# Two accumulator banks as two tiles instead of one in a fused recurrence and MLP kernel

## The chip, the cores and the metric

The kernel runs on one core of one Trainium2 chip. The metric is the device time of one execution in microseconds (us). The core has five engines that run side by side, each in its own order: TensorE (PE, matrix products), VectorE (DVE), ScalarE (ACT), GpSimd (POOL) and SyncE (SP, which issues most transfers). PE writes its products into an accumulator memory, PSUM, of eight banks; a bank holds 512 float32 numbers in each of 128 partitions. DVE and ACT read the products from there.

## The reference

Two blocks follow each other. The first is a gated linear recurrence over 768 tokens for 4 x 8 heads of width 48; the second is an MLP of 3072 tokens, 384 to 2048 to 384, with a quick GELU. All numbers are float32.

```
f = 1.0 / (1.0 + np.exp(-f_logit))
for t in range(S):
    state = f[:, :, t, :, None] * state + np.einsum('bhd,bhe->bhde', k[:, :, t], v[:, :, t])
    y[:, :, t] = np.einsum('bhd,bhde->bhe', q[:, :, t], state)
...
x = attn_out.transpose(0, 2, 1, 3).reshape(B * S, H * D)
h = x @ w_in
g = h * (1.0 / (1.0 + np.exp(-1.702 * h)))
return (g @ w_out).astype(np.float32)
```

## The kernel before

**Units.** The 3072 tokens are cut into twelve units (`NALL`) of 256 tokens (`U`), numbered 0 to 11. For each unit the kernel runs the recurrence ("attention") and then the MLP. The recurrence of a unit is done in chunks of 64 tokens: score products in six levels on PE (`score`, line 448), which DVE and ACT move under masks into a matrix A; then `add` (line 558) multiplies A with v into the accumulator y; the part "S" (line 669) makes the states at the chunk borders; the part "W" (line 716) adds what the states contribute to y. ACT then copies y to `yT` (line 731; line 768 in unit 11), transfers bring it into the layout `xT`, and POOL forms sums of it, called E (line 998).

**The MLP.** Units 0 to 2 run it with plain products. From unit 3 on its first layer (`mlp_h20`) is a scheme of twenty products for a 4 x 3 by 3 x 2 block product, with sums of blocks as operands. The table `PRODUCTS` names for each product its two operands, its parent (whose finished bank it adds onto) and the outputs it counts towards. `WHOLE` (units 3 to 10) and `HALVES` (unit 11, two groups) give the order on PE and put every product into a lane. `product` (line 1028) issues a product: PE at line 1036; a copy by ACT at line 1043 if a child goes on in another lane; then the reads: ACT at line 1055 for the first part of an output, DVE at line 1064 for the others, ACT at line 1051 where an output has a single part, and the GELU at line 1066. The second layer (`mlp_o7`, line 897, accumulators o_X, o_Y, o_Z, o_W) uses seven products in place of eight.

**PSUM.** All tiles come from one pool `ps`. Four tags, mm0 to mm3, hold one bank each; the function `bank` hands them out, and lanes 0 to 3 are these. The tag y is one tile of two banks, and so is sc. The tag y serves the scores of two levels in units 0 and 1, the accumulator of `add` in every unit (line 553, one bank for each group g of 128 tokens) and, in `mlp_h20`, lanes 4 and 5 (lines 1022 to 1025). The tag sc serves the scores, the state products, the last token's output (`y_last`, line 757), in unit 11 also lanes 6 and 7, and at the very end the product `o_last` (line 1161). A tile of a tag waits until the tile before it in the same tag has been read. In `mlp_h20` the lanes 4 and 5 of one unit are the two halves of one and the same tile:

```
tag = "y" if lane < 6 else "sc"
if tag not in shared:
    shared[tag] = ps.tile([P, 2, 512], F32, tag=tag, name=f"h_{n}_{tag}")
banks[lane] = shared[tag][:, lane % 2, :wide * w].rearrange("p (t x) -> p t x", x=w)
```

**What sets the order.** The orders of PE and POOL are written out by hand for the whole kernel (line 91): from unit 3 on, the parts of the next unit's attention are merged into the MLP's list of products by their widths. For units 0 to 2 the orders of all engines are written out (`fill_order`, closed at line 1386). After that the framework sets the order of DVE, ACT and SP at build time, by its own estimate of when each instruction can start, and it derives all semaphore waits from the tiles that instructions read and write. `half` copies y to `yT`: half(0) reads the bank of group 0 and a part of the other, half(1) the rest, later. In unit 11 fifteen operations on DVE (line 1103) and one at line 1101 build `sum_last`, the output of the last token, which PE turns over in `o_last` (line 1162). In attention, z (line 629) is the transpose of k that goes out to memory and comes back as `kt`, and ACT turns it into `kn` (line 644) for the products at line 669. The DVE transposes at line 367 bring in the next unit's inputs, and the products on X at line 546 scale them for each level.

Of the kernel before, what the change touches and what calls it, by code (L numbers as in the profile page):

```python
# [9 lines left out]
F32 = mybir.dt.float32  # L10
# [13 lines left out]
def kernel(  # L24
# [33 lines left out]
    nc = tc.nc  # L58
# [29 lines left out]
    wp = ctx.enter_context(tc.tile_pool(name="wp", bufs=2))  # L88
    mlp = ctx.enter_context(tc.tile_pool(name="mlp", bufs=2))
    ps = ctx.enter_context(tc.tile_pool(name="ps", bufs=1, space=bass.MemoryType.PSUM))  # L90
    ctx.enter_context(tc.manual_schedule(engines={mybir.EngineType.PE, mybir.EngineType.Pool}))
    fill_order = ExitStack()
    fill_order.enter_context(tc.manual_schedule())
# [244 lines left out]
    def attention(n):  # L338
# [124 lines left out]
        def columns(h, g):  # L463

            return rows(h ^ g)

        def scores(tag="sc"):
            new = ps.tile([P, 2, NP, 2, HS], F32, tag=tag, name=f"sc_{n}_{next(serial)}")
            t["sc"], t["both"] = (new[:, 0], new[:, 1]), [(0, new.rearrange("p h a s t -> p (h a) s t"))]
            return new  # L470

# [78 lines left out]
        def add():  # L550


            t["py"] = ps.tile([P, NG, NP, 2, HS], F32, tag="y", name=f"y_{n}")
            for a in range(NP):
                for f in (1, 0):
                    for h, g in TILES:
                        to, w = (slice(0, HS), HS) if h == g == 0 else (columns(h, g), D)
                        nc.tensor.matmul(
                            t["py"][to, g, a, f, :],
                            lhsT=vts[n][g * HS:(g + 1) * HS, f, (2 * a + h) * D:(2 * a + h) * D + w],  # L560
                            rhs=A[g * HS:(g + 1) * HS, h * NP + a, f, :],
                            start=(f == 1 and a == 0), stop=False, skip_group_check=True,
                        )
# [47 lines left out]
        def turn_k(a0):  # L611
            if a0 == 0:
                new_kn()
            if n < N_FILL + 1:
                pt = bank([P, 2, 2, P], f"tkn_{n}_{a0}")
            else:
                pt = ps.tile([P, 2, 2, P], F32, tag="sc", name=f"tkn_{n}_{a0}")
            for a in range(2):
                for f in range(2):
                    x = (a0 + a) * HALF  # L620
                    nc.tensor.transpose(pt[:, a, f, :], slot((KR, KF)[f])[:, x:x + HALF], ident)
            nc.scalar.copy(t["kn"][:, a0:a0 + 2], pt)
# [33 lines left out]
        @part("S")  # L656
        def _():
            if n:
                add()
                pd = scores().rearrange("p h a s t -> p h (a s t)")  # L660
                pd = [pd[:, g] for g in range(NG)]
            else:
                pd = [bank([P, NP * 2 * D], f"pd_{g}", g) for g in range(NG)]
            for a in range(NP):
                for f in (1, 0):
                    for h in range(2):
                        for g in range(NG):
                            x = (a * 2 + f) * D
                            nc.tensor.matmul(  # L669
                                pd[g][h * HS:(h + 1) * HS, x:x + D],  # L670
                                lhsT=t["kn"][g * HS:(g + 1) * HS, a, f, h * HS:(h + 1) * HS],
                                rhs=vts[n][g * HS:(g + 1) * HS, f, (2 * a + h) * D:(2 * a + h + 1) * D],
                                start=True, stop=True,
                            )
            if not n:
                units[1][0][2]()
                add()

                seen = t["py"][HS:HS + 1, 1, 0, 1, :1]
                nc.scalar.copy(seen, seen)  # L680
            if n != N_FILL - 1:
                load_v(n + 1)
            st = att.tile([P, NC, NP, D], F32, tag="st", name=f"st_{n}", bufs=2)
            D64 = t["tms"][NL].rearrange("p (f a g) -> p f g a", f=2, a=NP)
            prev = t["ahead"] = last.get("st")
            t["before"] = [prev[:, NC - 1] if c == 0 and not first else st[:, c - 1] if c else None for c in range(NC)]
            for c in range(NC):
                g, f = CHUNK[c]
                d = pd[g][:, :NP * 2 * D].rearrange("p (a f e) -> p f a e", a=NP, f=2)[:, f]
                if t["before"][c] is None:  # L690
                    nc.vector.tensor_copy(st[:, c], d)
                    continue
                by = D64[:, ORDER.index(f), g].unsqueeze(2).broadcast_to((P, NP, D))
                nc.vector.tensor_tensor(st[:, c], t["before"][c], by, ALU.mult)
                copied["state"] = nc.vector.tensor_tensor(st[:, c], st[:, c], d, ALU.add)
            last["st"] = st

        @part("W")
        def _():

            py = t["py"]
            for cs in ((1, 0), (2, 3)):
                for a in range(NP):
                    for c in cs:
                        g, f = CHUNK[c]
                        w = HS
                        if t["before"][c] is None:
                            if not n:  # L710
                                continue
                            w = 1
                        for h in range(2):
                            state = t["before"][c][rows(h), a] if w > 1 else t["ahead"][rows(h), NC - 1, a]
                            x = a * HALF + g * HS
                            nc.tensor.matmul(  # L716
                                py[columns(h, g), g, a, f, :w], lhsT=state, rhs=X[rows(h), query(n, f), x:x + w],
                                start=False, stop=True, skip_group_check=True,
                            )
            if n == NALL - 1:  # L720
                whole(py)
                return
            yT = att.tile([P, NP, NG, G], F32, tag="kn", name=f"yT_{n}", bufs=1)
            xT = mlp.tile([P, NK, width(n)], F32, tag="xT", name=f"xT_{n}", bufs=3)

            def half(h):
                for g in range(h, NG):
                    for f in (1, 0):
                        at, step = (g * HS, 1) if f else (U - 1 - g * HS, -1)
                        to, of = (rows(h), columns(h, g)) if g else (slice(0, HS + D),) * 2  # L730
                        nc.scalar.copy(view(yT[to], at, [[U, NP], [step, HS]]), py[of, g, :, f, :])  # L731
                two = ((nc.scalar, nc.sync), (nc.sync, nc.scalar))[n] if h and n < N_FILL else (nc.sync,)
                to_x(lambda h: (yT[rows(h), :NK], lambda r, d: yT[r:r + d, NK]), xT[:, :, :U], NG, (h,), two)
            half(0)
            if n > N_FILL and n < NALL - 1:
                xTs[n] = xT

                def rest():
                    with tc.issue_after(copied["aside"].ins):
                        half(1)  # L740
                    sums_of_x(n)
                return rest
            if n == N_FILL - 1:
                xTs[n] = xT
                return lambda: half(1)
            half(1)
            xTs[n] = xT
            if n > N_FILL:
                sums_of_x(n)

        def whole(py):
# [2 lines left out]
            yT = att.tile([P, NP, 1, w], F32, tag="kn", name=f"yT_{n}", bufs=1)  # L754
            xT = mlp.tile([P, NK, w], F32, tag="xT", name=f"xT_{n}", bufs=3)
            nc.gpsimd.memset(xT[:, :, U + 1:], 0.0)
            pl = ps.tile([P, NP], F32, tag="sc", name="y_last")
            for a in range(NP):
                for h in range(2):
                    nc.tensor.matmul(  # L760
# [3 lines left out]
            for h in range(2):  # L764
                for f in (1, 0):
                    for g in range(NG):
                        at, step = (g * HS, 1) if f else (U - 1 - g * HS, -1)
                        nc.scalar.copy(view(yT[rows(h)], at, [[w, NP], [step, HS]]), py[columns(h, g), g, :, f, :])
                nc.scalar.copy(yT[rows(h), :, 0, U], pl[rows(h)])
                to_x(  # L770
                    lambda h: (yT[rows(h), :NK, :, :U + 1], lambda r, d: yT[r:r + d, NK, :, :U + 1]), xT[:, :, :U + 1], 1, (h,)
# [231 lines left out]
    def mlp_h20(n, g, before):  # L1003
# [14 lines left out]
        def take(lane, name):  # L1018
            if lane < 4:
                banks[lane] = bank([P, wide, w], f"h_{n}_{name}", lanes["h"][lane])  # L1020
            else:
                tag = "y" if lane < 6 else "sc"
                if tag not in shared:
                    shared[tag] = ps.tile([P, 2, 512], F32, tag=tag, name=f"h_{n}_{tag}")
                banks[lane] = shared[tag][:, lane % 2, :wide * w].rearrange("p (t x) -> p t x", x=w)
            return banks[lane]

        def product(x, group, lane):
# [128 lines left out]
    def mlp_unit(n, fill):  # L1157
        g, before = {}, []

        def last_token():  # L1160
            po = ps.tile([P, DM], F32, tag="sc", name="o_last")
            nc.tensor.matmul(po[:1], lhsT=ones, rhs=g["last"][:, 0], start=True, stop=True)
            nc.scalar.copy(g["last"][:1, 0], po[:1])
            nc.sync.dma_start(out=out[NALL * U - 1:, :], in_=g["last"][:1, 0])
# [272 lines left out]
```

## Time and profile before

| | |
|---|---|
| three runs | 584.63, 584.95, 585.52 us; median 584.95 |
| the profiled execution | 586.86 us, of which the span of all instructions is 585.1 us |
| 0 to 171 us: units 0 to 2 and the first attention of unit 3 | PE busy 159.91 us |
| 171 to 520 us: units 3 to 10 | of 349.00 us PE busy 347.62, DVE 273.32, ACT 186.02, POOL 92.27 |
| 520 to 537 us: last attention, second layer of unit 10 | of 17.00 us PE busy 16.53 |
| 537 to 562.5 us: first layer of unit 11 | of 25.50 us PE busy 23.32, DVE 9.76, ACT 11.25 |
| 562.5 to 585.1 us: second layer of unit 11, output | of 22.60 us PE busy 19.32, DVE 14.23 |

A row of the timeline gives the start from the beginning of the span, the length, the engine, the line, the operation, the tiles (output<-inputs, numbers left out), the shapes and how many instructions are merged; in brackets stands the idle time of the engine before it and what ended it, where that is over 0.15 us. PE matmuls overlap, so the distance between starts tells more than the lengths. A row of waits gives the total in us, how many there were and the longest. The tiles of lanes 0 to 3 are called h, those of lanes 4 and 5 h_y, those of lanes 6 and 7 h_sc.

### The profile page before, as it was taken

How to read it: one execution, taken by the hardware profiler on the slowest of the kernel's cores; microseconds unless marked ns; L12 is line 12 of the kernel's file. 1: busy time of each engine (PE TensorE's matmuls, PEld its weight loads, DVE VectorE, ACT ScalarE, POOL GpSimd, SP SyncE). 2: the span in 40 equal slices, each digit the busy share in tenths (PEclk: the TensorE clock that was granted, in tenths of full speed). 3: DMA queues.
4: the chain of work that ended last, by engine and by line, in shares of the span. 5: the costliest groups of instructions: out<-in, count | busy, mean ns of one | idle time of the engine just before them, and what ended most of it. 6: DMA issues, size and time to landing. Idle time of an engine off the chain costs nothing.

```text
span 585.1 us, 18537 instructions
## 1 busy us (share of the span) xinstructions
PE 566.7 (97%) x7838; PEld 516.1 (88%) x7838; DVE 442.3 (76%) x697; ACT 289.3 (49%) x588; POOL 141.7 (24%) x226
## 2 busy tenths in 40 slices
PE   7989899999999999999999999999999999999997
PEld 6757676776889999999999999999999999998896
DVE  1899887996888886997786897786897786461284
ACT  4755544322543563663563563564563563552440
POOL 3030120605442601501501601502502503103000
DMA  7869695932453362362443353452451211001000
GB/s 184 192 167 240 151 258 132 241 79 71 104 137 75 103 148 59 97 154 68 122 117 69 93 135 89 111 128 59 120 130 43 64 39 29 29 2 30 26 1 29
DMA packets 86772, 60.34 MB, mean 103 GB/s; under 512 B 33505, under 2 KB 78465, under 8 KB 86689
## 3 DMA queue, kind: packets, MB, share of 16 engines
q1 hardware_dynamic: 86208, 58.57, 40.2%
q8 instruction: 62, 1.02, 0.7%
q10 hardware_dynamic: 481, 0.59, 0.4%
q14 instruction: 21, 0.17, 0.1%
HBM read 45.49 MB, written 8.91 MB: 93 GB/s over the span
## 4 chain that ended last, share of the span: by engine, by line
PE 67%; DVE 12%; DMA 9%; ACT 5%; SPq 3%; issue 2%; POOL 0%; ACTq 0%; DVEq 0%; POOLq 0%
PE h L1036 14%; PE o_Y L897 12%; PE o_Z L897 9%; PE sc L448 6%; PE h_y L1036 5%; PE o_X L897 5%; DMA bits<-in_moe_w_in_dram 4%; PE o_W L897 4%; PE h L1130 3%; PE o L1144 3%; DVE X L367 2%; PE y L716 2%; DMA raw<-in_q_dram 2%; PE sc L669 2%; DVE z L629 2%
## 5 line engine op out<-in xcount | busy, mean ns | idle before, releaser
L546 DVE TENSOR_TENSOR X<-X,tot 128x1024 f32<-128x1024 f32 x50 | 67.2, 1345 | 45.3 <-PE sc L448 37.4
L517 ACT COPY Kc<-X 128x512 f32<-128x512 f32 x72 | 48.2, 670 | 86.2 <-DVE X L546 66.2
L998 POOL TENSOR_TENSOR E<-xT 128x128 f32<-128x128 f32 (+1 forms) x36 | 17.1, 484 | 228.0 <-DMA xT<-yT 228.0
L1130 PE MATMUL h<-xT,w_in 128*128 128x256 f32 x288 | 66.1, 383 | 3.8 <-DMA xT<-yT 2.9
L1130 PEld LDWEIGHTS h<-xT,w_in 128*128 128x128 f32 x288 | 53.5, 190 | 14.0 <-issue 4.0
L1036 PE MATMUL h<-E,w_in 128*128 128x128 f32 (+1 forms) x476 | 62.8, 277 | 0.6 <-DVE g L1064 0.6
L1036 PEld LDWEIGHTS h<-E,w_in 128*128 128x128 f32 x476 | 57.4, 192 | 1.5 <-issue 0.9
L897 PE MATMUL o_Y<-T,S 128*128 128x192 f32 x320 | 57.7, 329 | 0.0
L1066 ACT ACTIVATE g<-g 128x512 f32<-128x512 f32 (+1 forms) x70 | 40.3, 589 | 28.3 <-DVE g L1064 28.2
L897 PEld LDWEIGHTS o_Y<-T,S 128*128 128x128 f32 x320 | 52.2, 190 | 0.6
L1064 DVE TENSOR_TENSOR g<-g,h 128x512 f32<-128x512 f32 (+1 forms) x58 | 35.9, 638 | 16.3 <-PE h L1036 14.8
L367 DVE STREAM_TRANSPOSE X<-raw 128x512 f32<-128x512 f32 x40 | 42.9, 1111 | 3.1 <-PE y L716 2.7
L1144 PE MATMUL o<-w_out,g 128*128 128x384 f32 x128 | 43.7, 491 | 0.1
L508 DVE COPY_PREDICATED A<-masks,sc 128x256 f32<-128x256 uint32 (+1 forms) x98 | 41.8, 504 | 0.1
L1144 PEld LDWEIGHTS o<-w_out,g 128*128 128x128 f32 x128 | 23.7, 190 | 14.8 <-issue 0.2
L731 ACT COPY yT<-y 48x256 f32<-48x256 f32 (+1 forms) x66 | 21.1, 370 | 29.3 <-PE y L716 28.9
L394 POOL TENSOR_SCALAR F<-F 128x1024 f32<-128x1024 f32 x10 | 12.3, 1228 | 87.6 <-ACT F L397 87.6
L1055 ACT ACTIVATE g<-h 128x512 f32<-128x512 f32 (+1 forms) x52 | 28.5, 576 | 9.6 <-PE h L1036 9.3
L448 PE MATMUL sc<-X,Kc 48*64 48x64 f32 x1344 | 28.1, 220 | 2.7 <-ACT Kc L517 1.1
L448 PEld LDWEIGHTS sc<-X,Kc 48*64 48x64 f32 x1344 | 24.0, 134 | 6.9 <-ACT Kc L517 3.1
L897 PE MATMUL o_X<-w_out,g 128*128 128x192 f32 x160 | 29.6, 331 | 0.5 <-ACT o_X L861 0.5
L1134 ACT ACTIVATE g<-h 128x256 f32<-128x256 f32 x48 | 17.2, 383 | 24.9 <-PE h L1130 24.7
(161 smaller groups left out, 1201.8 us busy)
## 6 DMA issues: line engine op xcount, KB each, us to landing
bits<-in_moe_w_out_dram SPq DMA_DIRECT2D x8, 768.0 KB
raw<-in_f_logit_dram SPq DMA_DIRECT2D x48, 96.0 KB
raw<-in_k_dram SPq DMA_DIRECT2D x48, 96.0 KB
bits<-in_moe_w_in_dram SPq DMA_DIRECT2D x8, 576.0 KB
raw<-in_q_dram SPq DMA_DIRECT2D x44, 96.0 KB
k_tok<-z SPq DMA_DIRECT2D x64, 64.0 KB
kt<-k_tok SPq DMA_DIRECT2D x16, 256.0 KB
out_dram<-osb SPq DMA_DIRECT2D x20, 192.0 KB
```

The lines of the kernel that those rows point to most:

```text
L367: nc.vector.transpose(view(out, at, [[HALF, NP], [step, R4], [R4 * step, 32]]), by_half[:, j, f].rearrange("p a (j d) -> p (a j) d", j=R4) ...
L448: nc.tensor.matmul(t["sc"][h][g * HS:(g + 1) * HS, a, s, :], lhsT=t["Kc", l][rows(h), x:x + HS], rhs=rhs(h, a, g), start=True, stop=True,)
L508: moved = nc.vector.copy_predicated(out=view(A, c * HALF + at, dims), mask=mask.bitcast(U32), data=got)
L517: nc.scalar.copy(c.rearrange("p (n two m) -> p n two m", two=2, m=m), view(X, KF * SLOT, [[2 * m, SLOT // (2 * m)], [(KR - KF) * SLOT + m, ...
L546: nc.vector.tensor_tensor(x, x, y, ALU.mult)
L897: nc.tensor.matmul(t[name], lhsT=lhs(f), rhs=rhs(f), start=(new and i == 0), stop=(i == HF - 1), skip_group_check=True,)
L1036: nc.tensor.matmul(ph[:, t], lhsT=WA[a][:, f // 2, f % 2 * P:(f % 2 + 1) * P], rhs=E[n][b], start=(root and t == 0), stop=not goes_on, ski ...
L1055: nc.scalar.activation(to, ph, AF.Copy, scale=float(sign))
L1064: copied["sum"] = nc.vector.tensor_tensor(to, to, part, ALU.add if sign > 0 else ALU.subtract)
L1066: nc.scalar.activation(to, to, AF.Gelu_apprx_sigmoid)
L1130: nc.tensor.matmul(ph, lhsT=w_in[:, ff // 2, c, ff % 2 * P:(ff % 2 + 1) * P], rhs=xTs[n][:, c, :], start=(c == 0), stop=(c == NK - 1))
L1144: nc.tensor.matmul(t["po"], lhsT=g[ff // FG][:, ff % FG, tt * P:(tt + 1) * P], rhs=w_out[:, ff, :], start=(ff == ffs[0]), stop=(ff == ffs[ ...
```

## The change

The tag y gets a pool of its own with a tile of two banks, which is opened at its first use. When `add` of unit 2 is reached, that pool is closed and another opened in the same place, whose tags y0 and y1 hold one bank each. From then on the accumulator of `add` is two tiles, one for each group, and in `mlp_h20` every root product or copy that takes lane 4 or 5 gets a new tile of its own bank. The tag sc gets a pool of its own too; it is exchanged in the same way when unit 11's first layer takes lane 6 for the first time. From there lanes 6 and 7 are tiles of sc0 and sc1, and `o_last` is a tile of sc0. Products, copies, reads, their sizes and the order written out by hand stay as they are.

```diff
+    two_banks, pools, side = {}, {}, {"y": "left", "sc": "right"}
+
+    def psum_pool(tag, apart=False):
+
+        if tag not in two_banks:
+            two_banks[tag] = ctx.enter_context(ExitStack())
+            pools[tag] = two_banks[tag].enter_context(tc.tile_pool(name=f"ps_{tag}", bufs=1, space=bass.MemoryType.PSUM, side=side[tag]))
+        if apart and (tag, 1) not in pools:
+            two_banks[tag].close()
+            pools[tag, 1] = ctx.enter_context(tc.tile_pool(name=f"ps_{tag}_apart", bufs=1, space=bass.MemoryType.PSUM, side=side[tag]))
+        return pools[(tag, 1) if apart else tag]
+
+    def one_bank(tag, i, name):
+        return psum_pool(tag, True).tile([P, 512], F32, tag=f"{tag}{i}", name=name)
...
         def scores(tag="sc"):
-            new = ps.tile([P, 2, NP, 2, HS], F32, tag=tag, name=f"sc_{n}_{next(serial)}")
+            new = psum_pool(tag).tile([P, 2, NP, 2, HS], F32, tag=tag, name=f"sc_{n}_{next(serial)}")
...
-            t["py"] = ps.tile([P, NG, NP, 2, HS], F32, tag="y", name=f"y_{n}")
+            if n < N_FILL:
+                py = psum_pool("y").tile([P, NG, NP, 2, HS], F32, tag="y", name=f"y_{n}")
+                t["py"] = [py[:, g] for g in range(NG)]
+            else:
+                t["py"] = [
+                    one_bank("y", g, f"y_{n}_{g}").rearrange("p (a f t) -> p a f t", a=NP, f=2) for g in range(NG)
+                ]
...
-            pl = ps.tile([P, NP], F32, tag="sc", name="y_last")
+            pl = psum_pool("sc").tile([P, NP], F32, tag="sc", name="y_last")
...
                 tag = "y" if lane < 6 else "sc"
-                if tag not in shared:
-                    shared[tag] = ps.tile([P, 2, 512], F32, tag=tag, name=f"h_{n}_{tag}")
-                banks[lane] = shared[tag][:, lane % 2, :wide * w].rearrange("p (t x) -> p t x", x=w)
+                if tag == "y" or n == NALL - 1:
+                    new = one_bank(tag, lane % 2, f"h_{n}_{name}")
+                else:
+                    if tag not in shared:
+                        shared[tag] = psum_pool(tag).tile([P, 2, 512], F32, tag=tag, name=f"h_{n}_{tag}")
+                    new = shared[tag][:, lane % 2]
+                banks[lane] = new[:, :wide * w].rearrange("p (t x) -> p t x", x=w)
...
-            po = ps.tile([P, DM], F32, tag="sc", name="o_last")
+            po = one_bank("sc", 0, "o_last")[:, :DM]
```

The other lines of the diff only follow from these: `py[..., g, ...]` becomes `py[g][...]` where y is written and read, and the tile of `turn_k` (line 617) comes from `psum_pool("sc")`.

More of the change, by code (lines that the diff above doesn't have):

```diff
@@ L558, in add @@
                         nc.tensor.matmul(
-                            t["py"][to, g, a, f, :],
+                            t["py"][g][to, a, f, :],
                             lhsT=vts[n][g * HS:(g + 1) * HS, f, (2 * a + h) * D:(2 * a + h) * D + w],
@@ L616, in turn_k @@
             else:
-                pt = ps.tile([P, 2, 2, P], F32, tag="sc", name=f"tkn_{n}_{a0}")
+                pt = psum_pool("sc").tile([P, 2, 2, P], F32, tag="sc", name=f"tkn_{n}_{a0}")
             for a in range(2):
@@ L677, in _ @@
                 add()
-                seen = t["py"][HS:HS + 1, 1, 0, 1, :1]
+                seen = t["py"][1][HS:HS + 1, 0, 1, :1]
                 nc.scalar.copy(seen, seen)
@@ L716, in _ @@
                             nc.tensor.matmul(
-                                py[columns(h, g), g, a, f, :w], lhsT=state, rhs=X[rows(h), query(n, f), x:x + w],
+                                py[g][columns(h, g), a, f, :w], lhsT=state, rhs=X[rows(h), query(n, f), x:x + w],
                                 start=False, stop=True, skip_group_check=True,
@@ L730, in half @@
                         to, of = (rows(h), columns(h, g)) if g else (slice(0, HS + D),) * 2
-                        nc.scalar.copy(view(yT[to], at, [[U, NP], [step, HS]]), py[of, g, :, f, :])
+                        nc.scalar.copy(view(yT[to], at, [[U, NP], [step, HS]]), py[g][of, :, f, :])
                 two = ((nc.scalar, nc.sync), (nc.sync, nc.scalar))[n] if h and n < N_FILL else (nc.sync,)
@@ L767, in whole @@
                         at, step = (g * HS, 1) if f else (U - 1 - g * HS, -1)
-                        nc.scalar.copy(view(yT[rows(h)], at, [[w, NP], [step, HS]]), py[columns(h, g), g, :, f, :])
+                        nc.scalar.copy(view(yT[rows(h)], at, [[w, NP], [step, HS]]), py[g][columns(h, g), :, f, :])
                 nc.scalar.copy(yT[rows(h), :, 0, U], pl[rows(h)])
```

## The prediction

> **What bounds the kernel.** I read the page's busy times first, then who TensorE (PE) waits for, then the timeline of PE beside VectorE (DVE) and ScalarE (ACT) in one middle unit and in the last one.
>
> ```profile
> PE 566.7 (97%) x7838; PEld 516.1 (88%) x7838; DVE 442.3 (76%) x697; ACT 289.3 (49%) x588; POOL 141.7 (24%) x226
> ```
>
> PE is the bound: of 349.0 us between 171 and 520 it is busy 347.62 us, at a granted clock of 1.00 throughout. Only what PE itself waits for can be won. Its named waits at the lines of the change are few:
>
> ```profile
> PE h_sc L1036 <- DVE g L1064: 0.9, 1, 0.9
> PE h_y L1036 <- ACT g L1051: 0.5, 1, 0.5
> PE h_y L1036 <- ACT g L1055: 0.5, 1, 0.5
> ```
>
> The attention chain on DVE is in turn paced by PE: its longest wait is for scores.
>
> ```profile
> DVE X L546 <- PE sc L448: 37.4, 22, 3.2
> ```
>
> Waits under 0.15 us are not listed by name, so I looked at the pitch of PE's products. In a middle unit (unit 3) a product of eight instructions takes 0.89 us from start to start, but not here (columns: start, length, engine, line, operation):
>
> ```profile
> 202.09 1.06 PE L1036 MATMUL h<-E,w_in 128*128 128x128 f32 x8
> 203.10 1.16 PE L1036 MATMUL h_y<-xT,w_in 128*128 128x128 f32 x8
> 204.09 1.06 PE L1036 MATMUL h<-E,N_p 128*128 128x128 f32 x8
> ...
> 202.36 0.69 DVE L1064 TENSOR_TENSOR g<-g,h_y 128x512 f32<-128x512 f32 x1 [0.57 <-PE h_y L1036]
> ...
> 198.77 0.57 ACT L1043 COPY h_y<-h_y 128x512 f32<-128x512 f32 x1 [0.35 <-PE h_y L1036]
> ```
>
> The product at 203.10 is number 14 in `PRODUCTS`, in lane 4. Its own bank was last touched by the ACT copy that read it (over at 199.34). It starts 0.05 us after DVE has read product 19, which lies in lane 5: the other bank of the same tile. From 202.09 to 204.09 go 2.00 us where two pitches are 1.78. So a wait goes by the tile, not by the bank. The last unit proves it:
>
> ```profile
> 547.48 0.61 PE L1036 MATMUL h_y<-xT,w_in 128*128 128x129 f32 x4
> 548.63 0.71 PE L1036 MATMUL h_y<-xT,N_p 128*128 128x129 f32 x4 [0.54 <-ACT g L1051]
> 549.18 0.61 PE L1036 MATMUL h<-E,N_p 128*128 128x129 f32 x4
> ...
> 555.24 0.61 PE L1036 MATMUL h_sc<-E,w_in 128*128 128x129 f32 x4
> 556.71 0.71 PE L1036 MATMUL h_sc<-xT,w_in 128*128 128x129 f32 x4 [0.86 <-DVE g L1064]
> 557.26 0.61 PE L1036 MATMUL h<-xT,w_in 128*128 128x129 f32 x4
> ...
> 548.19 0.39 ACT L1051 ACTIVATE g<-h_y 128x258 f32<-128x258 f32 x1
> ...
> 556.24 0.41 DVE L1064 TENSOR_TENSOR g<-g,h_sc 128x258 f32<-128x258 f32 x1
> ```
>
> Line 1051 reads only products whose output has one part; there is one, product 5, here in lane 5. Yet product 12 in lane 4 waits for it. Likewise product 5 of the other half, in lane 6, waits for DVE's read of product 7 in lane 7. No data goes between them.
>
> **The change part by part.** *Middle units.* In `WHOLE` the only product that follows a reader of the other bank closely is number 14. PE starts it late in units 3 to 9 (203.10, 246.84, 290.54, 334.32, 378.05, 421.31, 465.02), each time by 2.00 - 1.78 = 0.22 us (0.12 of waiting, 0.10 because the first instruction after a wait takes 378 ns instead of 275). In unit 10 (508.56) transposes stand between and nothing is lost. With two tiles number 14 waits only for the copy 3.6 us earlier. That gives 7 x 0.22 = 1.54 us on PE. Does it stay won? PE's next real waits are for `kn` (260.93, 348.44, 435.42) and for DVE's read of a lane that the change leaves alone (211.68, 299.17). The chain of waits back from these runs through the delayed product itself in units 3, 4, 5 and 8 (DVE reads it, then transposes z), so what released them comes earlier too; in units 7 and 9 no wait follows. Only in unit 6 does the chain pass by (a DVE copy at 329.88, then the z transfer). I take 6 x 0.22 = 1.32 us, bounds 0 and 1.54.
>
> *Last unit.* Here a product is four instructions, pitch 0.445 us (557.26, 557.70, 558.15, 558.60). Six products wait for the other bank of their tile. From the start of the one before to the start of the one after, less 0.89:
> - 540.50, product 14, lane 5, for ACT's read of lane 4: 1.68, so 0.79
> - 548.63, product 12, lane 4, for lane 5: 1.70, so 0.81
> - 550.71, product 13, lane 6, for ACT's read of lane 7: 1.19, so 0.30
> - 554.24, product 19, lane 4, for DVE's read of lane 5: 1.29, so 0.40
> - 556.71, product 5, lane 6, for lane 7: 2.02, so 1.13
> - 559.29, product 3, lane 5, for DVE's read of lane 4: 1.24, so 0.35
>
> Sum 3.78 us: 2.35 from y, 1.43 from sc. What each needs in its own bank was over at 538.68, 544.27, 545.59, 552.32, 551.88 and 554.19, at least 1.1 us before it could start at full pitch, and moves earlier with PE. A seventh late product (546.93, 0.26) waits for an output sum in another lane and stays.
>
> *What is late next.* DVE has to follow. Its idle stretches at 554.99, 557.88 and 560.04 (0.80, 0.70, 0.81) all end with PE or with ACT's read of a PE product, so they take up the 1.88 us that PE gains after 552 (the 1.90 before it come through as an earlier start). From 560 on DVE is full up to the end of `sum_last` at 576.16; PE needs that at 578.22, 2.06 us later, with PE gaining at most 3.78 and DVE nearly as much. I take no loss; if DVE did not move, it would be the third rival.
>
> *At nothing.* The products, copies and reads stay as many, and PE's and POOL's order is written out in the program, so it stays. SP, the DMA queues and the loads get nothing new. Closing the two-bank pool of y falls before `add` of unit 2 (PE 120.31); the last reader of y of unit 1 ends at 67.36, 53 us of cover. Closing that of sc falls before product 0 at 537.17; `y_last` was read by 527.14. A new tile per root or copy waits for the readers of the same bank, a subset of what the pair waited for. `add` (215.99) and product 17 (197.62) show no wait for y before. The last term is the order on ACT, DVE and SP, which is not written out after unit 2 and is made anew when waits change: from below 0 (the four `kn` and two DVE waits of the middle, about 0.5 us each with their restart, 3.1 in all, vanish) to a loss (fourth rival). I take 0, as the queues' inputs move by 0.2 us a unit, less than one 0.69 us DVE read.
>
> The Trainium skill ("TensorE: Matmul & The Clock Gate", sections "Single matmul latency" and "Back-to-back issue gap") prices what a lone matmul cannot hide at (398 + N)/2.4 less N/2.4 + 2.5, some 163 ns. By that estimate 13 stops would give back 2.1 us instead of the 1.3 that the 378 ns rows show, and the time would be near 579.1; I go by the rows.
>
> **Sum.** 1.32 + 3.78 = 5.10 us of the profiled execution (span 585.1 us, 586.86 with what lies around it, which the change does not touch): span 580.0, execution 581.8. The runs' median of 584.95 lies 1.9 below that execution; taken off it, **579.9 us**.
>
> **Rivals.**
> 1. *The middle gives nothing* (0.13): the next real wait swallows the 0.22 each time, since `kn` hangs on the z transfer. For it: four `kn` waits of 0.24 to 0.34 us; against: the chain through the delayed product. 584.95 - 3.78 = 581.2.
> 2. *The waits stay* (0.07): the framework also orders tiles of one pool, or each new tile brings the same wait. Against: lanes 0 to 3 are such tiles and show no wait for each other's readers. 585.0.
> 3. *DVE's tail* (0.08): DVE moves only by the 1.32 of the middle, `sum_last` ends at 574.84, and the last unit gives no more than its slack of 2.06. 584.95 - 3.38 = 581.6. Against: DVE's idle stretches.
> 4. *Slower* (0.06): the order on DVE and ACT turns so that z goes behind two more reads of 0.69 us and `kn` comes 1.38 later; with slack near zero where PE already waits for it, 7 units x 1.38 = 9.7 lost, 5.1 won: 589.5. It decides from 5.1/7 = 0.73 us a unit on, so from more than one read. For it: behind the second z DVE's order already differs between unit 3 (207.03 to 211.75) and unit 4 (250.76 to 254.18); against: no unit loses more than 0.5 us.
> 5. *Better order* (0.06): the 3.1 us of the middle go as well: 576.8.
>
> **Numbers.** Forecast 0.60, its own range 578.7 to 580.9 (below: unit 6's 0.22 and two of the middle's waits of 0.5 as well; above: three quarters of the middle's term lost). With rivals 1 and 3 that is 0.81; the high end is rival 3's 581.6 and the 0.89 by which the runs shown differ, 582.5, the low end 578.6. About 0.2% (1.2 us) is what can be told from no change. Faster: 0.60 + 0.13 + 0.08 + 0.06 = 0.87; same 0.07; slower 0.06.
>
> **What would show it.** The new tiles go by the name h, so h_y and h_sc vanish from the rows. Number 14 should follow its predecessor at 0.89 in every middle unit; the stretch from the first lane-6 product to the last product (537.17 to 562.07, 24.90 us) should shrink to 21.1; PE's waits for L1051 and L1055 should go, the one for the output sum stay; `o_last` should start without a wait. Wrong would be: waits on lanes 4 to 7 that remain, longer waits for `kn`, or DVE's `sum_last` released last.

## The result and the profile after

| | before | after |
|---|---|---|
| runs | 584.63, 584.95, 585.52, 585.61 us | 579.53, 580.93, 581.46, 581.59 us |
| median | 585.24 us | 581.19 us |
| profiled execution, span | 586.86 us, 585.1 us | 579.53 us, 577.7 us |

The ratio of the times is 0.9914, with a 95% interval of 0.9893 to 0.9936, which is 3.7 to 6.3 us faster (the medians alone give 0.9931, inside it). In later runs (e1 below) the changed kernel took 580.26 us against 585.92, ratio 0.9904 (0.9875 to 0.9933). Lines of the changed file stand 14 to 24 higher: 448 is now 462, 669 is 689, 897 is 917, 1036 is 1060, 1064 is 1088.

First the busy times of the changed kernel, to be read against those of before:

```profile
span 577.7 us, 18535 instructions
## 1 busy us (share of the span) xinstructions
PE 562.1 (97%) x7838; PEld 514.0 (89%) x7838; DVE 440.9 (76%) x697; ACT 289.2 (50%) x588; POOL 143.6 (25%) x226
```

As many matmuls as before, and the same share of a shorter span. PE's waits for others, out of the list for the changed kernel (total, times, longest), those after the opening:

```profile
PE sc L689 <- ACT kn L664: 1.0, 4, 0.3
...
PE h L1060 <- DVE g L1088: 0.5, 2, 0.3
...
PE o_X L917 <- ACT o_X L881: 0.3, 1, 0.3
```

The three waits on h_y and h_sc are gone and none has come in their place; the waits for `kn`, for DVE's read of a lane and for o_X were there before (1.1, 0.6 and 0.5). Unit 3 in the timeline of PE, at the place of product 14:

```profile
201.21 1.06 PE L1060 MATMUL h<-xT,w_in 128*128 128x128 f32 x8
202.10 1.06 PE L1060 MATMUL h<-E,N_p 128*128 128x128 f32 x8
203.00 1.06 PE L1060 MATMUL h<-xT,w_in 128*128 128x128 f32 x8
```

Product 14 (201.21) is followed at 0.89 us, and is no longer 1.16 but 1.06 long: the slow first instruction after a wait has gone too. The last unit's first layer, products 5 and 12 and then products 7 and 5:

```profile
543.13 0.61 PE L1060 MATMUL h<-xT,w_in 128*128 128x129 f32 x4
543.58 0.61 PE L1060 MATMUL h<-xT,N_p 128*128 128x129 f32 x4
544.03 0.61 PE L1060 MATMUL h<-E,N_p 128*128 128x129 f32 x4
...
549.39 0.61 PE L1060 MATMUL h<-E,w_in 128*128 128x129 f32 x4
549.84 1.06 PE L1060 MATMUL h<-xT,w_in 128*128 128x129 f32 x8
```

They start 0.45 us apart where 1.15 and 1.47 us lay between them. ACT's read of product 5 runs beside them, in the other bank:

```profile
543.84 0.39 ACT L1075 ACTIVATE g<-h 128x258 f32<-128x258 f32 x1
```

**Where the 7.4 us of the two profiled spans come from.** PE executes the same 7838 matmuls in the same order, so the two traces can be laid over each other instruction by instruction. At the state products of unit 3 the changed kernel is already 1.77 us ahead, before any tile that a middle unit splits has been waited for; that part is not the change (the experiments show it). From there to the first of the last sixteen matmuls:

| stretch, from start to start | before | after | won |
|---|---|---|---|
| state products of unit 3 to the scores of unit 11 in unit 10's first layer | 170.58 to 500.68 | 168.81 to 497.28 | 1.63 us |
| to the o_X products of unit 10 | to 527.52 | to 523.96 | 0.16 us |
| to the last sixteen matmuls | to 578.95 | to 571.63 | 3.76 us |
| together | 408.37 | 402.82 | 5.55 us |

The steps sit where the prediction had them: 0.22 us at product 14 of each of units 3 to 9, and six steps in unit 11.

### The profile page after: what moved, and what is told of

Its sections match the earlier page's. It is cut to its first block, busy times and chain, and to the rows that moved or that the text cites. A ratio compares the mean times of both kernels' runs of the same rounds, so it can differ in the third digit from the quotient of the medians.

```text
span 577.7 us, 18535 instructions
## 1 busy us (share of the span) xinstructions
PE 562.1 (97%) x7838; PEld 514.0 (89%) x7838; DVE 440.9 (76%) x697; ACT 289.2 (50%) x588; POOL 143.6 (25%) x226
## 4 chain that ended last, share of the span: by engine, by line
PE 66%; DVE 14%; DMA 8%; ACT 5%; SPq 3%; issue 3%; POOL 1%; ACTq 0%; DVEq 0%; POOLq 0%
PE h L1060 19%; PE o_Y L917 11%; PE o_Z L917 8%; PE sc L462 6%; PE o_X L917 5%; PE o_W L917 4%; PE h L1154 3%; PE o L1168 3%; DVE X L381 3%; DMA bits<-in_moe_w_in_dram 2%; DVE X L560 2%; PE y L736 2%; DVE z L649 2%; PE sc L689 2%; DMA raw<-in_q_dram 1%
## 5 line engine op out<-in xcount | busy, mean ns | idle before, releaser
L560 DVE TENSOR_TENSOR X<-X,tot 128x1024 f32<-128x1024 f32 x50 | 65.8, 1316 | 44.5 <-PE sc L462 34.7
L1060 PE MATMUL h<-E,w_in 128*128 128x128 f32 (+1 forms) x648 | 83.0, 276 | 0.5 <-DVE g L1088 0.5
L1060 PEld LDWEIGHTS h<-E,w_in 128*128 128x128 f32 x648 | 77.1, 192 | 1.4 <-issue 0.9
L1088 DVE TENSOR_TENSOR g<-g,h 128x512 f32<-128x512 f32 (+1 forms) x92 | 55.4, 626 | 26.3 <-PE h L1060 17.7
L1079 ACT ACTIVATE g<-h 128x512 f32<-128x512 f32 (+1 forms) x70 | 37.1, 550 | 12.8 <-PE h L1060 10.9
L1060 PE MATMUL h<-E,N_c 128*128 128x128 f32 (+1 forms) x288 | 37.1, 275 | 0.0
L408 POOL TENSOR_SCALAR F<-F 128x1024 f32<-128x1024 f32 x10 | 14.3, 1429 | 86.6 <-ACT F L411 86.6
L1060 PEld LDWEIGHTS h<-E,N_c 128*128 128x128 f32 x288 | 35.1, 192 | 0.2 <-DVE osb L877 0.2
```

Of the source, the lines that this page charges most:

```text
L560: nc.vector.tensor_tensor(x, x, y, ALU.mult)
L1060: nc.tensor.matmul(ph[:, t], lhsT=WA[a][:, f // 2, f % 2 * P:(f % 2 + 1) * P], rhs=E[n][b], start=(root and t == 0), stop=not goes_on, ski ...
L1079: nc.scalar.activation(to, ph, AF.Copy, scale=float(sign))
L1088: copied["sum"] = nc.vector.tensor_tensor(to, to, part, ALU.add if sign > 0 else ALU.subtract)
```

## Experiments

Theory T: the framework makes an instruction wait for the readers of the whole tile it writes, so PE stood for readers of the other bank. Rivals: O, the gain comes from an order of ACT and DVE made anew; P, from where the banks lie; W, PE waits for the lane's own data; S, a part of the profiled gap is the opening of the kernel. Each run is given as the median against the kernel before on the same chip, and as the stretch from the state products of unit 3 to the last sixteen matmuls (408.37 us before), which leaves the opening out.

| run | median, before | ratio (95% interval) | stretch | against before |
|---|---|---|---|---|
| e1, changed kernel again | 580.26, 585.92 | 0.9904 (0.9875 to 0.9933) | 402.83 | -5.54 |
| e2, y only | 582.07, 585.92 | 0.9932 (0.9907 to 0.9957) | 404.32 | -4.05 |
| e3, sc only | 584.47, 585.92 | 0.9974 (0.9957 to 0.9991) | 406.69 | -1.68 |
| e4, pools only | 585.95, 585.92 | 1.0001 (0.9984 to 1.0018) | 408.34 | -0.03 |
| e5, y in unit 11 only | 584.58, 586.85 | 0.9964 (0.9950 to 0.9978) | 406.12 | -2.25 |
| e6, other order, no split | 584.58, 586.85 | 0.9962 (0.9949 to 0.9975) | 407.45 | -0.92 |
| e7, changed, two more waits off | 579.78, 586.85 | 0.9884 (0.9870 to 0.9899) | 402.07 | -6.30 |
| e8, e7 and two products before `kn` | 592.38, 586.85 | 1.0100 (1.0073 to 1.0126) | 412.04 | +3.67 |
| e9, the same, counted | 581.94, 586.63 | 0.9916 (0.9901 to 0.9930) | 403.14 | -5.23 |
| e10, one product, counted | 580.29, 586.63 | 0.9894 (0.9878 to 0.9909) | 403.11 | -5.26 |

**e1, the changed kernel again.**

> The changed kernel once more, for its scatter and for a second profile. Theory T (a wait goes by the tile, so PE stood for readers of the other bank): from the state products of unit 3 to the end PE is again 5.5 us shorter than before, and only what comes ahead of unit 3 differs between two profiles; median of the runs 579.5 to 581.5, ratio 0.990 to 0.994. Rival S (a part of the profiled gap of 7.4 us is the start): the 1.67 us that the first changed profile was ahead at unit 3 comes and goes from profile to profile. If the 5.5 us themselves shrink in this profile, T has the wrong size.

The stretch is the same to 0.01 us (402.82 and 402.83), while the lead at unit 3 is 0.88 us here and was 1.77. So S holds for that part, and the 5.5 do not come from the opening.

**e2, y only**, against the changed kernel:

```diff
-                if tag == "y" or n == NALL - 1:
+                if tag == "y":
...
-            po = one_bank("sc", 0, "o_last")[:, :DM]
+            po = psum_pool("sc").tile([P, DM], F32, tag="sc", name="o_last")
```

> Only y is split, sc stays one tile of two banks in unit 11 too. T: the waits of lanes 4 and 5 go (seven of 0.22 us in units 3 to 9; 0.79, 0.81, 0.40 and 0.35 in unit 11), the two of lanes 6 and 7 stay (0.30 and 1.13): gain 1.54 + 2.35 = 3.9 us, near 581.3. Rival O (the gain comes from an order of ACT and DVE made anew): the gain does not split by tile, and the two sc waits change with it.

**e3, sc only:**

```diff
-            if n < N_FILL:
+            if True:
...
-                if tag == "y" or n == NALL - 1:
+                if tag == "sc" and n == NALL - 1:
```

> Only sc is split, in unit 11; y stays one tile of two banks. T: the two waits of lanes 6 and 7 go, gain 0.30 + 1.13 = 1.4 us, near 583.8; the 0.22 us of product 14 stays in every middle unit, and the four waits of lanes 4 and 5 in unit 11 stay. Rival O: as much as both together, or nothing.

**e4, pools only:**

```diff
-            if n < N_FILL:
+            if True:
...
-                if tag == "y" or n == NALL - 1:
+                if False:
...
-            po = one_bank("sc", 0, "o_last")[:, :DM]
+            po = psum_pool("sc").tile([P, DM], F32, tag="sc", name="o_last")
```

> y and sc have pools of their own, on the same sides as in the changed kernel, but both stay tiles of two banks throughout. T: all 13 waits stay, no gain (within 0.2%, 584.5 to 585.7). Rival P (the place of the banks or the exchange of pools helps): some of the 5 us appears without any split.

PE's waits at the first layer, out of the lists of e2, e3 and e4 in this order:

```profile
PE h_sc L1060 <- DVE g L1088: 0.9, 1, 0.9
```

```profile
PE h_y L1060 <- ACT g L1075: 0.5, 1, 0.5
PE h_y L1060 <- ACT g L1079: 0.5, 1, 0.5
```

```profile
PE h_sc L1060 <- DVE g L1088: 0.9, 1, 0.9
...
PE h_y L1060 <- ACT g L1075: 0.5, 1, 0.5
PE h_y L1060 <- ACT g L1079: 0.5, 1, 0.5
```

Each split takes off the waits of its own pair and leaves those of the other pair standing; without a split all stay, to 0.03 us in the stretch. That settles O and P: neither the pools nor their places do anything. It settles W too, because the products, their data and PE's order are the same in all of these kernels. It also agrees with the executed order in the trace of the changed kernel: DVE has one of its 697 instructions in another place (a sum S in unit 11), ACT two of the first three yT copies swapped in each of units 2 to 10 and one swap in unit 11. Sizes: y 4.05 (forecast 1.54 + 2.35 = 3.89, the rest is the 0.16 at o_X), sc 1.68 (forecast 1.43). The sc split is worth 0.25 more by itself because in e3 product 3 of lane 5, which lost 0.35 before, starts in step although y is unsplit:

```profile
556.49 1.06 PE L1060 MATMUL h<-E,w_in 128*128 128x129 f32 x8
557.38 0.70 PE L1060 MATMUL h_y<-E,w_in 128*128 128x129 f32 x4
```

0.89 us for the two products before it is the full pitch. With the sc waits off, the read that held it came earlier against it. With y alone split, on the other hand, product 5 of lane 6 waits 0.06 us longer than before (0.92 in place of 0.86). So the two splits overlap by 4.05 + 1.68 - 5.55 = 0.18 us, about 0.25 less 0.06.

**e5, y in unit 11 only:** e4 with the line

```diff
-                if False:
+                if tag == "y" and n == NALL - 1:
```

> y is split for the first layer of unit 11 alone; in units 2 to 10, and for add in every unit, it stays one tile, and so does sc. Theory T: the 0.22 us of product 14 stays in units 3 to 9, the four waits of lanes 4 and 5 in unit 11 go: gain 2.3 us against before. With the kernel that splits y everywhere (3.9) that leaves 1.6 for the middle. A rival in which the middle units' gain comes through the yT copies of add, or in which the last unit's is an end effect of a faster middle, would put this near 0 or near 3.9.

2.25 us, near the 2.35 worked out for the four waits of lanes 4 and 5: all four are gone, and product 5 of lane 6 waits 0.06 us longer, as in e2. e2 less e5 leaves 1.80 us for the middle units and o_X, where the table above has 1.63 + 0.16. So the gain of unit 11 does not hang on the middle units, nor theirs on it.

**e6, another order on PE, no split**, against the kernel before:

```diff
-        (14, 4), (4, 2), (5, 0), (10, 5), (6, 3), (3, 2), (8, 1), (12, 5), (16, 3), (11, 2),
+        (4, 2), (14, 4), (5, 0), (6, 3), (10, 5), (3, 2), (8, 1), (12, 5), (16, 3), (11, 2),
...
-        (26, 0), (27, 7), (5, 6), (14, 3), (10, 4), (9, 2), (29, 7), (3, 5), (36, 0), (31, 1),
+        (26, 0), (27, 7), (14, 3), (10, 4), (5, 6), (9, 2), (29, 7), (3, 5), (36, 0), (31, 1),
```

> The kernel before, tiles unsplit, with the order on PE changed so that a product comes later than the reader of the other bank: in units 3 to 10 products 4 and 14 change places, and 10 and 6; in unit 11 product 5 of lane 6 comes two places later. T: product 14 starts when the read of product 19 is over, so its 0.22 us goes from most of units 3 to 9, and most of the 1.13 us of product 5 as well; gain 1.5 to 2.7 us without any split, less what product 10 now waits for the read of 14. Rival W (PE waits for the lane's own data): the waits move along with the products and nothing is gained.

The median says 2.3 us less (1.5 to 3.0 by the interval), the trace 0.92 from unit 3 on. The trace leaves out the opening, in which this profile is 1.55 us ahead, so its figure is used here; why the interval of the medians lies above it stays open. Two places of e6 on PE, unit 3 and unit 4:

```profile
201.45 1.06 PE L1036 MATMUL h<-E,N_p 128*128 128x128 f32 x8
202.34 1.06 PE L1036 MATMUL h_y<-xT,w_in 128*128 128x128 f32 x8
203.24 1.06 PE L1036 MATMUL h<-xT,w_in 128*128 128x128 f32 x8
```

```profile
244.00 1.06 PE L1036 MATMUL h<-E,w_in 128*128 128x128 f32 x8
245.72 1.13 PE L1036 MATMUL h<-E,N_p 128*128 128x128 f32 x8 [0.67 <-ACT h L1043]
246.69 1.06 PE L1036 MATMUL h_y<-xT,w_in 128*128 128x128 f32 x8
```

Product 14 now starts without a wait in units 3 to 10 with the tile unsplit, as T has it. This does not part T from W, though, since the product comes 0.89 us later and its own data would be ready too; what speaks against W is e2 to e4. But product 4, put in its place, waits for ACT's copy into lane 2, a wait for data, in units 4 and 6 (0.83 and 0.62 us over the pitch, 0.07 for the restart each), and that, with some smaller waits, eats the 1.5 us. What stays is the gain of unit 11, where product 5 gives back 0.90 us. The expectation (1.5 to 2.7 us) fits in kind and was too high for the middle.

**e7, two more waits off**, against the changed kernel:

```diff
-            nc.scalar.copy(t["X"], t["Y"])
+            if n == NALL - 2:
+                nc.vector.tensor_copy(t["X"], t["Y"])
+            else:
+                nc.scalar.copy(t["X"], t["Y"])
...
-        (15, 6), (30, 4), (33, 1), (22, 0), (18, 3), (-1, -1), (1, 7), (20, 2), (25, 5), (32, 4), (24, 1),
+        (15, 6), (30, 4), (33, 1), (22, 0), (18, 3), (-1, -1), (1, 7), (25, 5), (20, 2), (32, 4), (24, 1),
```

> The changed kernel with two further edits: in unit 10 the copy of o_Y to o_X is made by DVE instead of ACT, where it stands behind eight yT copies, and in unit 11 product 5 of lane 5 goes ahead of product 0 of lane 2, which waits for the output sum. T: these are the last waits of PE after unit 10 (0.48 and 0.10 us, 0.16 and 0.10): up to 0.8 us faster than the changed kernel. If DVE is late with the copy behind its sums, nothing or a loss.

The stretch is 0.75 us shorter than the changed kernel's, of 0.84 at stake; by the medians this is the fastest of all, 7.1 us under the kernel before. DVE makes the copy behind its sums (0.36 us at 524.06) and is done just before PE needs it at 524.54.

**e8, two products between `add` and the state products**, against e7. The edit holds for units 4 to 10, one more than its expectation names:

```diff
                 add()
+                if n in CARRY and n > N_FILL + 1:
+                    for _ in range(2):
+                        fill.pop(0)[1]()
                 pd = scores().rearrange("p h a s t -> p h (a s t)")
```

> The kernel of e7 with two products of the second layer put between add and the state products in units 5 to 10, 0.65 us of PE work at the place where PE waits for kn (0.44 us and 0.07 of restart in units 5, 7 and 9). If kn is late by a fixed time against PE, the wait is covered: 1.5 us faster than e7. If what makes kn is paced by PE's later products, the wait comes back elsewhere and the time is that of e7.

It lost 10 us of stretch against e7. Its longest new wait, out of the list:

```profile
PE h L1066 <- POOL E L1024: 4.7, 5, 1.3
```

The products taken were not counted, so the list of products ran two further ahead in every unit, until PE stood at the first layer before POOL had made the sums E. Neither outcome named beforehand came.

**e9 and e10, the same counted**, with two products and with one:

```diff
+                        w, emit, _ = fill.pop(0)
+                        emit()
+                        state["pulled"] = state.get("pulled", 0) + w
...
             fn()
+            done += state.pop("pulled", 0)
```

> As e8, in units 4 to 10, but the two products put between add and the state products are counted, so that the list of products runs no further ahead of attention than in e7: PE reaches the first layer, and with it the sums E of POOL, at the time it did in e7. If e8's loss of some 10 us came from the list running ahead (PE then waits for E), it vanishes here, and with kn late by a fixed time against PE the time is up to 1.5 us below e7's, near 578.3 at e7's start. If the state products themselves must not be late, the loss stays.

> As e9 with one product, 0.33 us of PE work, between add and the state products: covers most of the 0.44 us that PE waits for kn in units 5, 7 and 9, so 1.0 us at most below e7. If e9 gains 1.5, this gains about two thirds of it; if e9 loses, half of its loss.

No wait for E any more, and in units 5, 7 and 9 none for `kn` either; yet both are about 1.05 us slower than e7 in the stretch. The place in e7 and in e9 (unit 5), PE:

```profile
258.32 1.14 PE L578 MATMUL y<-A,vt 64*64 64x64 f32 x64
259.73 1.15 PE L689 MATMUL sc<-vt,kn 64*64 64x48 f32 x64 [0.27 <-ACT kn L664]
```

```profile
260.34 1.14 PE L578 MATMUL y<-A,vt 64*64 64x64 f32 x64
261.41 0.92 PE L925 MATMUL o_W<-T,g 128*128 128x192 f32 x4
262.26 1.15 PE L694 MATMUL sc<-vt,kn 64*64 64x48 f32 x64
```

From y to the state products are 1.41 us with the wait, and 1.92 with two products worth 0.65: the wait of 0.47 goes and 0.33 comes, where PE turns from 64x64 pieces to whole products and back once more. In start-to-start distances over the pitch the turn to o_W costs 0.13 + 0.10 us and the one to the state products 0.09 + 0.02, together about 0.35 in each of seven units. (From y to the product behind the state products are 3.00 us, 0.65 of them for the two products, and 1.99 in the units of e7 that have no wait.) In units 5, 7 and 9 the wait with its restart (0.47 + 0.02) was a little dearer, in units 4, 6, 8 and 10 there was nothing to save: 4 x 0.35 - 3 x 0.14 = 1.0, near the 1.05 measured. That one product loses as much as two (2.67 us from y on, 0.33 of them for the product, so 0.35 again) fits: the turns are paid, not the products. Of the expectations the part on e8's loss held, as it vanished here; the gains expected of e9 and e10 did not come.

## Why the prediction was right

The forecast was 579.9 us with 578.6 to 582.5 around it; 581.19 and, again, 580.26 were measured. Its 5.10 us are 5.55 in the trace. The first median lies just above the forecast's own range, which ended at 580.9, and on the 581.2 of rival 1, so the median alone could not have told the two apart; the trace does, as the middle did give its 1.63 us.

- *A wait goes by the tile, not by the bank.* Right: e2, e3 and e4 turn each group of waits off and on with the split of its own pair, with products, data and PE's order unchanged.
- *Last unit, 3.78 us.* 3.76 measured, and the stretch from the first lane-6 product to the last product is 21.14 us, as forecast (21.1). That DVE would follow was right too: it ends `sum_last` at 568.83 and PE needs it at 570.89, again 2.06 us later, so rival 3 did not come.
- *Middle, 1.32 us.* Mis-sized: 1.63. All seven units kept their 0.22, which is 1.54; of the rest, 0.06 comes from a shorter wait for DVE in unit 5 (299.17). The step that failed is "Only in unit 6 does the chain pass by": the wait for `kn` that follows it nearly kept its size (0.47 us over the pitch before, 0.45 after), so what made `kn` came earlier as well. The rows of before show a way: the second z of that unit stands on DVE right behind the read of the product after number 14, for which DVE waited on PE. No run tests that link by itself.

```profile
336.47 0.69 DVE L1064 TENSOR_TENSOR g<-g,h 128x512 f32<-128x512 f32 x1 [0.26 <-PE h L1036]
337.07 1.15 DVE L629 STREAM_TRANSPOSE z<-X 128x512 f32<-128x512 f32 x1
```

- *`add`, product 17 and the yT copies at nothing.* Right for PE's waits of these; but 0.16 us were won at o_X of unit 10, where PE waits for ACT behind the yT copies of unit 11. With two tiles the first four copies end 1.40 us after their start, where they took 1.51, which is 0.11 of the 0.16:

```profile
520.29 1.40 ACT L788 COPY yT<-y 48x256 f32<-48x256 f32 x4 [4.20 <-PE y L736]
```

- *The order on ACT, DVE and SP at nothing.* Right: practically unchanged, so rivals 4 and 5 did not come. Rival 5 was priced too high: of its four waits for `kn` one (170.58) lies ahead of the middle, and the other five waits came to about 2.5 us, not 3.1; all but 0.1 of that stayed.
- *The price of a restart.* By the rows 13 stops give back 0.10 us each, and the overlay of the two traces shows 0.10 at the second matmul of each of the 13. All seven units by the rows, with the 0.16 at o_X, make 1.54 + 3.78 + 0.16 = 5.48, and 5.55 was measured: the rows hold. By the estimate from the Trainium skill ("TensorE: Matmul & The Clock Gate", "Single matmul latency" and "Back-to-back issue gap") a stop would give back 0.16, which would add 0.8 to the sum; the trace does not agree with it.
- *The profiled execution*, forecast at 581.8 us, took 579.53, mostly because its opening was 1.77 us ahead; the larger gain (5.55 for 5.10) is the rest.

## What to carry to other kernels

Where two buffers that are used independently are halves of one tile, look in the trace for an instruction that starts within 0.05 us of the end of a read of the other half: that wait is only bookkeeping, and a tile for each half removes it. Add the start-to-start distances against the full pitch, since waits under 0.15 us are not listed and each costs a slow restart besides (0.10 us here). A wait on the busiest engine is worth filling only if what fills it brings no extra change of operation there, and every piece of work pulled forward has to be counted in the plan.

## What the runs showed of the hardware

- The opening differs from one execution to the next. In the twelve profiles the same matmul, the first state product of unit 3, starts between 168.47 and 171.42 us, with kernels that are alike up to there but for the pools and the tiles of y. One part is TensorE: its 96 opening transposes took 8.32 us in the profile of before and 7.04 in that of the changed kernel, because their pitch halves at about 10.3 us in the one and 8.3 in the other, though the profile gives the granted clock as 1.00 in both there. In the profile of e1 the granted clock was 0.79 between 12 and 20 us (the row below: the stretch, its length, the busy times of PE, weight loads, DVE, ACT and POOL, the clock, the transfers' share and GB/s). The Trainium skill ("TensorE: Matmul & The Clock Gate", "What's actually happening") says that the array starts at half rate and that the moment it is released varies from run to run, by 500 ns either way; the pitches agree with that in kind, but the two moments here lie 2.0 us apart. Another part is transfers: PE waited 1.06 us for xT ahead of the first MLP products of before (40.48), and not at all in the changed kernel (39.13). So runs of one kernel scatter by 2 us and more (23 runs of the kernel before: 584.02 to 588.89), while the stretch inside a trace came out alike to 0.01 us in two profiles of the changed kernel.

```profile
12.00:20.00 8.00, 6.77 (x152) 4.84 (x151) 4.54 (x7) 4.16 (x10) 0.65 (x2) 0.79 0.70 159
```

- A turn of PE from 64x64 pieces to whole products and back to pieces costs 0.35 us (e9, e10). The Trainium skill ("TensorEngine Tiling (Array Packing)", "Key Properties") says that a change of the tiling mode drains the array and names no price; the runs fit that and give one, though none of them shows the drain by itself.
